# Another form of the seven products for the second MLP product: four sums instead of five, four banks instead of three, 21 quarters by seven

## The chip, the cores and the metric

The kernel runs on one core of one Trainium2 chip. The metric is the device time of one execution in microseconds; lower is better. TensorE does the matrix products, VectorE (DVE) and ScalarE (ACT) the elementwise work, GpSimd (POOL) and SyncE (SP) issue the transfers. A matrix product is written to one of eight accumulation banks (PSUM), each of 2 KB per partition, which is 512 float32 values; ACT and DVE read the banks.

## The reference, cut to what matters

```python
scores = scale * q @ k.T                     # 8 batches, 8 heads, 576 positions, 64 wide
ret    = scores * gamma ** (i - j)           # for i >= j, else 0; gamma by head
x      = (ret @ v), heads side by side       # 4608 tokens x 512
h      = x @ w_in                            # 512 x 2048
g      = 0.5 * h * (1 + erf(h / sqrt(2)))
out    = g @ w_out                           # 2048 x 512, float32
```

## The kernel before, in words

The 4608 tokens are nine blocks of 512. For each block the attention part gives `x` (by chunks of 128 positions with a running state), the first MLP product gives `h`, the gelu gives `g`, and the second MLP product gives the output. All weights stay in SBUF as bf16; `q`, `k`, `v` are loaded chunk by chunk through POOL's queue in the order of the list `ORDER`, and outputs are stored through SP's queue.

Some products are done "by seven": a product of 2 x 2 sub-blocks needs eight sub-products, and Strassen's scheme in Winograd's form needs seven, with sums of the inputs before and sums of the products after. The second MLP product is done so for blocks 1 to 8 (function `fast`): rows are cut into two halves of 256 tokens, columns into two halves of 256, and each of the seven products is two pieces, one for each 128 rows `r`, of eight matmuls of 256 columns. The two pieces of a product write the two halves of one bank, a tile of 128 x 2 x 256 float32; only in the last block has each row a bank of its own (`rows_at_once`). The first MLP product of a block is four quarters (`kp`), and a quarter is done plainly ("p" in `LAYOUTS`, 16 matmuls of 512 columns in `mlp1`) or by seven (a digit in `LAYOUTS`, 28 matmuls of 256 columns in `unit`). In `LAYOUTS` of before, blocks 2 to 8 have 2, 3, 2, 3, 2, 3 and 3 quarters by seven, 18 in all, and 10 plain ones.

In the second product of before, the products run in the order 3 2 1 5 4 6 7 on three banks Y, Z and X. Five sums of `g` (`g_sum`, ten DVE instructions a block) and five sums of `w_out` (`w_sum`, once) come before. After them `add_chain` puts a chain: product 3 is copied to SBUF (`third`), product 2 is taken from it (`less`), product 1 added (`more`), product 5 taken away (`dif`), and the four quadrants of the output are copied (`quadrant`) or added (`c11`) into the output buffer `o_sb`. Every one of these steps waits for both rows of a product, and reads the bank as 128 x 512 in one instruction.

The order of the instructions on each engine is fixed before the run by a planner written into the kernel (`Plan`, `pe_candidates`). It gives every operation a duration, a due time and what it depends on, and emits operations in the order of their planned start; TensorE's stream of MLP pieces may be taken out of order within a look-ahead of `LOOK` pieces, and attention work is put between them. The kernel sets no semaphore itself: the tile framework, in manual order, puts in the waits that the order of emission and the tiles touched call for. For the first 16 us the planner fills TensorE's gaps with matmuls on zeros (`warm`).

Of the kernel before, what the change touches and what calls it, by code (L numbers as in the profile page):

```python
# [9 lines left out]
FP32 = mybir.dt.float32  # L10
# [88 lines left out]
def kernel(  # L99
# [31 lines left out]
    for bp in range(B // 2):  # L131
        for ci in range(0 if bp > 1 else 1, NCI - 1):
# [12 lines left out]

    N_PE_TR = 10
    N_LD = 8
    N_QKT = 6
    N_VH = 5
    N_RET = 3  # L150
    N_Q = 3
    VH_ACT = [5, 8, 9, 10, 16, 18, 20, 24, 25, 29, 30, 33, 34, 37]
    HOT = 9.2
    N_WARM = 8
    SLACK = 0.05
    CUTS = (0, 128, 256, 384, 512)
    AHEAD = 5
    VH_DUE = 14.0
    FAST = 1
    UNIT_FROM = 2  # L160
    LOOK = 6
    HOLD = 4.7
    LAYOUTS = {2: ['2p3', '0', 'p1'], 3: ['0', '12', 'p3'], 4: ['01', 'p2', 'p3'], 5: ['0', '12', 'p3'], 6: ['32', 'p0', 'p1'], 7: ['01', '2', 'p3'], 8: ['0', '12', 'p3']}
    LEAD = 18.0
    SPREAD = 4.4
    EASE = 8.9
    ORDER = ("pos k1 q2 q1 k2 q3 v1 k3 v2 wi0 wi4 v3 q5 wi1 wi5 q4 wi2 wi6 wi3 k5 k4 wi7 wo0 v4 v5 wo4 wo1 wo5 k6 "
             "wo2 wo6 k9 q9 v8 k7 wo7 wo3 q7 q6 k10 v6 q8 v7 k8 q10 v9 v10").split()
    K_ORDER = [0, 1, 8, 9, 2, 3, 10, 11, 4, 5, 12, 13, 6, 7, 14, 15]
    PRODUCTS = "3215467"  # L170
    LAYOUT = {t: ["p0", "p1", "p2", "p3"] for t in range(2, N_BLK)}
    for t in range(UNIT_FROM, N_BLK):
        LAYOUT[t] = LAYOUTS[t]
# [80 lines left out]
    for t in range(N_BLK):  # L254
        if t < 2:
            cuts = CUTS if t == 0 else (0, 256, 512)
            for lo, hi in zip(cuts, cuts[1:]):
                stream.append([("1", t, m, 2, lo, hi) for m in K_ORDER[::2]])
        else:
            stream.append([one for block in LAYOUT[t] for one in laid(t, block)])  # L260
        if t < FAST:
            stream.append([("2", t, ts, m, m + 2) for m in range(0, N_DF, 2) for ts in range(2)])
            stream.append([("2", t, ts, m, m + 4) for ts in range(2, 4) for m in range(0, N_DF, 4)])
        else:
            stream.append([("2", t, p, r, n) for n, p in enumerate(PRODUCTS) for r in range(2)])

    def piece_time(one):
        if one[0] == "u":
# [398 lines left out]
    LEFT = {"2": 0, "1": 1, "5": 2, "6": 3, "7": 4}  # L667
    RIGHT = {"3": 0, "1": 1, "4": 2, "6": 3, "7": 4}
    BEHIND = {"5": "m3", "4": "q", "6": "dif", "7": "c21"}

    def g_of(t, m):
        kp = m % 8 // 2
# [7 lines left out]
    def g_sum(t, two, which):  # L680
        if which == 0:
            s_ring[two].take()
            s_tiles[t, two] = s_pool.tile([128, 3, 4, HALF], BF16, tag=f"s{two}", name="s")
        s_t = s_tiles[t, two]
        g = g_tiles[t, two].rearrange("p a b h s -> p (a b) h s")
        a11, a12 = g[:, :, 0, :HALF], g[:, :, 1, :HALF]
        a21, a22 = g[:, :, 0, HALF:], g[:, :, 1, HALF:]
        out_, x0, x1, op = ((s_t[:, 0], a21, a22, ALU.add), (s_t[:, 1], a11, a22, ALU.add),
                            (s_t[:, 2], a11, a12, ALU.add), (a21, a21, a11, ALU.subtract),
                            (a12, a12, a22, ALU.subtract))[which]  # L690
        nc.vector.tensor_tensor(out_, x0, x1, op=op)  # L691

    def w_sum(kp, which):
        if kp not in w_sums:
            w_sums[kp] = const.tile([128, 5, 2, 256], BF16, name=f"w_sum{kp}")
        hi, lo = w_out_sb[kp], w_out_sb[kp + 4]
        b11, b12, b21, b22 = hi[:, :, :256], hi[:, :, 256:], lo[:, :, :256], lo[:, :, 256:]
        x0, x1, op = ((b12, b22, ALU.subtract), (b11, b22, ALU.add), (b21, b11, ALU.subtract), (b11, b12, ALU.add),
                      (b21, b22, ALU.add))[which]
        nc.vector.tensor_tensor(w_sums[kp][:, which], x0, x1, op=op)  # L700

    for kp in range(4):
        for which in range(5):
            add(f"ws{kp}.{which}", "dve", 0.335, [f"land wo{kp}", f"land wo{kp + 4}"],
                lambda kp=kp, which=which: w_sum(kp, which), begins["2", FAST] - 6 + kp)

    def left(t, p, kp):
        if p in "215":
            return s_tiles[t, kp // 2][:, LEFT[p], kp % 2 * 2:kp % 2 * 2 + 2]
        g = g_tiles[t, kp // 2][:, kp % 2]  # L710
        return {"3": g[:, :, 0, :HALF], "4": g[:, :, 1, HALF:], "7": g[:, :, 1, :HALF], "6": g[:, :, 0, HALF:]}[p]

    def right(p, kp):
        if p == "2":
            return w_out_sb[kp][:, :, :256]
        if p == "5":
            return w_out_sb[kp + 4][:, :, 256:]
        return w_sums[kp][:, RIGHT[p]]


    wi_sums, xs_tiles, first_again = {}, {}, {}
# [92 lines left out]
    def chain_of(key, shape, n):  # L814
        c = chain.setdefault(key, {})
        if n not in c:
            c[n] = bank(shape, FP32, {"Y": "yT", "X": "xT_", "Z": "zT"}[n])
        return c[n][1]

    def unit(one):  # L820
# [14 lines left out]
    def fast(one):  # L835
        _, t, p, r, _ = one
        rs = next(x for x in rows_at_once(t) if r in x)
        c = chain_of(("2", t, rs), [128, len(rs), HALF], BANK_OF[p])
        at = r - rs[0]
        for kp in range(4):  # L840
            for kk in range(2):
                nc.tensor.matmul(c[:, at, :], lhsT=left(t, p, kp)[:, kk, r * 128:r * 128 + 128],  # L842
                                 rhs=right(p, kp)[:, kk, :], start=(p in "321" and at + kp + kk == 0),
                                 stop=(kp == 3 and kk == 1), skip_group_check=True)
        if p == PRODUCTS[-1] and r == 1:
# [59 lines left out]
    def c11(key):  # L905
        z = chain[key]["Z"][1]
        to = z if key[0] == "u" else target(key, "c11")
        nc.vector.tensor_tensor(to, chain[key]["q"], z, op=ALU.add)  # L908
        m_ring.give(T["dve"] + 0.12)
        if key[0] == "2":  # L910
            go(key, "Z", T["dve"] + 0.12)

    def add_chain(key, width, pe, due):

# [43 lines left out]
    for run in stream:  # L958
        for one in run:
# [18 lines left out]
            elif isinstance(one[2], str):  # L978
# [4 lines left out]
                if p in LEFT:  # L983
                    deps += [f"gs{t},{two}.{LEFT[p]}" for two in range(2)]
                if p in "34":
                    deps += gelus_of(t, range(4), int(p == "4"))
                deps += [f"ws{kp}.{RIGHT[p]}" for kp in range(4)] if p in RIGHT else []
                deps += [f"land wo{kp + 4 * (p == '5')}" for kp in range(4)] if p in "25" else []
                deps += [key + BEHIND[p]] if p in BEHIND else []
                add(nm, "pe", piece_time(one), deps, lambda one=one: fast(one), W[one], DRAIN,  # L990
                    banks=int(p in "321" and r == rs[0]))
                if p == PRODUCTS[-1] and r == rs[-1]:
                    at_ = {q_: {x: W["2", t, q_, x, PRODUCTS.index(q_)] for x in rs} for q_ in PRODUCTS}
                    add_chain(("2", t, rs), len(rs), {q_: [f"mlp{('2', t, q_, x, PRODUCTS.index(q_))}" for x in rs] for q_ in PRODUCTS},
                              {q_: max(at_[q_].values()) for q_ in PRODUCTS})
                    if t < N_BLK - 1:
                        add(f"st{t},1", "sp", 1.1, [key + "c21", key + "c22"], lambda t=t: store(t, 1), W[one])
                        add(f"st{t},0", "sp", 1.1, [key + "c12", key + "c11"], lambda t=t: store(t, 0), W[one] + 1)
                    else:
                        add(f"st{t},1.{r}", "sp", 0.5, [key + "c21", key + "c22"],  # L1000
                            lambda t=t, r=r: store(t, 1, slice(None), (r,), ends=False), W[one])
                        add(f"st{t},0a.{r}", "sp", 0.5, [key + "c12"],
                            lambda t=t, r=r: store(t, 0, slice(256, 512), (r,), ends=False), W[one])
                        add(f"st{t},0.{r}", "sp", 0.5, [key + "c11"],
                            lambda t=t, r=r: store(t, 0, slice(0, 256), (r,), ends=False), W[one] + 1)
            else:
                _, t, ts, n0, n1 = one
                ms = K_ORDER[n0:n1]
# [10 lines left out]
    for t in range(FAST, N_BLK):  # L1019
        for two in range(2):  # L1020
            kps = [2 * two, 2 * two + 1]
            gl = gelus_of(t, kps, 0) + gelus_of(t, kps, 1)
            for which in range(5):
                add(f"gs{t},{two}.{which}", "dve", 0.6, gl + ([f"gs{t},{two}.{which - 1}"] if which else []),
                    lambda t=t, two=two, which=which: g_sum(t, two, which),
                    begins["p", t, "21567"[which]] - 1.5 + 0.6 * two,
                    at=s_ring[two].at if not which else None)
    for kp in ever:
        over = [f"mlp{o}" for o in W if o[0] == "2" and o[1] == 0]
# [104 lines left out]
    def begun(one):  # L1134
# [2 lines left out]
            return one[3] in "321" or BANK_OF[one[3]] in chain.get(one[:3], ())  # L1137
        if one[0] == "2" and isinstance(one[2], str):
            rs = next(x for x in rows_at_once(one[1]) if one[3] in x)
            return (one[2] in "321" and one[3] == rs[0]) or BANK_OF[one[2]] in chain.get(("2", one[1], rs), ())  # L1140
        return True

    def pe_candidates():
# [113 lines left out]
```

## Time and profile before

| what | value |
|---|---|
| time, median of 3 runs | 287.55 us (286.61 to 287.65) |
| the profiled execution's own time | 285.85 us |
| its span, first to last instruction | 284.0 us |
| mean granted TensorE clock | 0.998 |
| TensorE busy | 278.8 us, 98% |
| DVE busy | 230.7 us, 81% |
| ACT busy | 174.6 us, 61% |
| POOL busy | 110.2 us, 39% |

The profiled execution lies 1.70 us under the median of the runs, and 1.9 us of its own time lie outside its span. A busy TensorE is counted from the start of a matmul to the modelled end of it, and matmuls are pipelined, so the spacing of the matmuls says more than the busy share.

### The profile page before, as it was taken

How to read it: one execution, taken by the hardware profiler on the slowest of the kernel's cores; microseconds unless marked ns; L12 is line 12 of the kernel's file. 1: busy time of each engine (PE TensorE's matmuls, PEld its weight loads, DVE VectorE, ACT ScalarE, POOL GpSimd, SP SyncE). 2: the span in 40 equal slices, each digit the busy share in tenths (PEclk: the TensorE clock that was granted, in tenths of full speed). 3: DMA queues.
4: the chain of work that ended last, by engine and by line, in shares of the span. 5: the costliest groups of instructions: out<-in, count | busy, mean ns of one | idle time of the engine just before them, and what ended most of it. 6: DMA issues, size and time to landing. Idle time of an engine off the chain costs nothing.

```text
span 284.0 us, 7609 instructions
## 1 busy us (share of the span) xinstructions
PE 278.8 (98%) x3080; PEld 219.9 (77%) x3080; DVE 230.7 (81%) x442; ACT 174.6 (61%) x396; POOL 110.2 (39%) x139
## 2 busy tenths in 40 slices
PE   7999999999999999999999999999999999999995
PEld 2689757588887688868875888688858887788684
DVE  4951775799999996979978999799789869939871
ACT  8678624797268735685377627884688258326921
POOL 8967778983566373508106467050000000000000
PEclk9999999999999999999999999999999999999999
DMA  9999999999999999999927999998310040003013
GB/s 151 159 182 189 187 181 162 193 193 135 136 146 184 178 131 129 149 214 156 178 84 41 154 159 225 144 147 70 148 37 6 0 148 3 2 11 139 0 35 115
DMA packets 151939, 35.49 MB, mean 125 GB/s; under 512 B 140896, under 2 KB 147552, under 8 KB 151904
## 3 DMA queue, kind: packets, MB, share of 16 engines
q0 software_dynamic: 115792, 17.97, 99.5%
q1 hardware_dynamic: 35072, 16.78, 32.8%
q8 instruction: 24, 0.39, 0.6%
q10 hardware_dynamic: 1040, 0.26, 0.4%
q14 instruction: 11, 0.09, 0.1%
HBM read 36.70 MB, written 9.44 MB: 162 GB/s over the span
## 4 chain that ended last, share of the span: by engine, by line
PE 60%; DVE 0%; issue 0%; DVEq 0%
PE zT L842 12%; PE hT L783 10%; PE yT L842 7%; PE zT L825 7%; PE yT L825 5%; PE o_ps L536 2%; PE sc L500 2%; PE o_ps L572 2%; PE xT__4502 L842 1%; PE xT__3131 L842 1%; PE xT__4102 L842 1%; PE xT__2624 L842 1%; PE xT__3636 L842 1%; PE u_ps L550 1%; PE xT__2163 L842 1%; PE xT__4807 L842 1%
## 5 line engine op out<-in xcount | busy, mean ns | idle before, releaser
L783 PE MATMUL hT<-xT,w_in 128*128 128x128 bf16 (+2 forms) x544 | 68.1, 279 | 0.0
L790 ACT ACTIVATE g<-hT 128x512 bf16<-128x512 f32 (+1 forms) x88 | 44.9, 527 | 16.9 <-PE hT L783 15.2
L842 PEld LDWEIGHTS <-g 128*128 128x128 bf16 x512 | 49.7, 98 | 7.0 <-issue 0.3
L783 PEld LDWEIGHTS <-w_in 128*128 128x128 bf16 x544 | 42.3, 98 | 16.3
L842 PEld LDWEIGHTS <-s 128*128 128x128 bf16 x384 | 37.4, 98 | 4.3
L412 POOL DMA_DIRECT2D qk_ld<-in_q_dram x31 | 27.9, 900 | 31.2 <-PE u_ps L550 19.0
L825 PEld LDWEIGHTS <-wi_sum 128*128 128x128 bf16 x360 | 35.1, 98 | 5.9 <-issue 0.2
L511 DVE TENSOR_TENSOR ret<-sc,msk 128x512 bf16<-128x512 f32 x56 | 36.1, 679 | 4.0 <-PE sc L500 4.0
L412 POOL DMA_DIRECT2D v_ld<-in_v_dram x31 | 27.9, 899 | 14.2 <-DMA qk_ld<-in_q_dram 4.8
L691 DVE TENSOR_TENSOR s<-g 128x1024 bf16<-128x1024 bf16 x48 | 31.5, 681 | 0.3 <-ACT g L899 0.3
L412 POOL DMA_DIRECT2D qk_ld<-in_k_dram x31 | 28.0, 902 | 8.4 <-DMA v_ld<-in_v_dram 4.7
L842 PE MATMUL zT<-w_sum,g 128*128 128x256 bf16 x256 | 30.7, 273 | 0.0
L524 ACT ACTIVATE vh<-v_ld,dv 128x64 bf16<-128x64 bf16 x104 | 26.5, 336 | 0.1
L899 ACT ACTIVATE g<-zT 128x512 bf16<-128x512 f32 x36 | 21.1, 629 | 2.7 <-DVE zT L908 2.7
L464 ACT COPY o_sb<-yT 128x512 f32<-128x512 f32 (+1 forms) x9 | 4.8, 538 | 28.6 <-PE yT L842 21.7
L464 ACT CAST u_sb<-u_ps 64x512 bf16<-64x512 f32 x29 | 16.8, 579 | 7.9 <-PE u_ps L550 7.0
L691 DVE TENSOR_TENSOR g<-g 128x1024 bf16<-128x1024 bf16 x32 | 21.3, 680 | 0.0
L464 ACT COPY q<-yT 128x512 f32<-128x512 f32 (+1 forms) x22 | 12.1, 572 | 13.7 <-PE yT L825 8.6
L587 DVE TENSOR_TENSOR xT<-o_ps,dqT 128x512 bf16<-128x512 f32 x28 | 18.2, 680 | 1.8 <-PE o_ps L572 1.7
L878 DVE TENSOR_TENSOR q<-q,zT 128x512 f32<-128x512 f32 (+1 forms) x27 | 17.5, 661 | 2.3 <-PE zT L825 1.3
L462 DVE COPY qkT<-qk_ps 128x512 bf16<-128x512 bf16 x14 | 5.9, 423 | 16.2 <-PE qk_ps L475 16.2
L908 DVE TENSOR_TENSOR zT<-q,zT 128x512 f32<-128x512 f32 x18 | 11.9, 692 | 6.7 <-PE zT L825 3.6
(199 smaller groups left out, 479.9 us busy)
## 6 DMA issues: line engine op xcount, KB each, us to landing
out_dram<-o_sb SPq DMA_DIRECT2D x30, 256.0 KB, 3.8
qk_ld<-in_k_dram POOLq DMA_DIRECT2D x31, 128.0 KB, 9.1
qk_ld<-in_q_dram POOLq DMA_DIRECT2D x31, 128.0 KB, 8.5
v_ld<-in_v_dram POOLq DMA_DIRECT2D x31, 128.0 KB, 8.9
w_in<-in_moe_w_in_dram POOLq DMA_DIRECT2D x8, 256.0 KB, 8.4
w_out<-in_moe_w_out_dram POOLq DMA_DIRECT2D x8, 256.0 KB, 8.6
out_dram<-o_sb SPq DMA_DIRECT2D x12, 128.0 KB, 2.3
qk_ld<-in_k_dram POOLq DMA_DIRECT2D x8, 64.0 KB, 6.5
```

Source lines behind the costliest of these rows:

```text
L412: nc.gpsimd.dma_start(dst, src[2 * bp + j, :, ci * C:ci * C + C, :].rearrange("h s d -> s h d"))
L464: nc.scalar.copy(dst, src)
L511: nc.vector.tensor_tensor(r, t, by, op=ALU.mult)
L524: nc.scalar.activation(vh[:, h], loaded[i][1][:, h], AF.Copy, scale=dv[:, h, ci:ci + 1])
L587: nc.vector.tensor_tensor(dst, o, by, op=ALU.mult)
L691: nc.vector.tensor_tensor(out_, x0, x1, op=op)
L783: nc.tensor.matmul(hT[:, m, :], lhsT=w[:, cc, o:o + 128], rhs=x_of(t)[:, cc, lo:hi], start=(cc == 0), stop=(cc == N_DM - 1))
L790: nc.scalar.activation(g_of(t, m0)[:, m0 % 2:m0 % 2 + n, m0 // 8, lo:hi], hT, AF.Gelu)
L825: nc.tensor.matmul(c[:, m, :], lhsT=unit_left(kp, p, m)[:, cc, :], rhs=unit_right(t, p)[:, cc, :], start=(p in "321" and m + cc == 0), sto ...
L842: nc.tensor.matmul(c[:, at, :], lhsT=left(t, p, kp)[:, kk, r * 128:r * 128 + 128], rhs=right(p, kp)[:, kk, :], start=(p in "321" and at + ...
L878: nc.vector.tensor_tensor(q_, q_, chain[key]["Z"][1], op=ALU.subtract)
L899: nc.scalar.activation(target(key, what), chain[key][n][1], AF.Gelu)
```

## The change

The second MLP product gets another form of the seven products. The sums of `g` are four (eight DVE instructions a block) and the sums of `w_out` are four; products 1, 2 and 3 take `w_out` as it is. The order is 1 2 6 7 4 5 3 on four banks: A holds product 1 and then product 2 on top of it, B product 6 and then 5, C product 7 and then 4, D product 3. Product 1 is copied by ACT, row by row, to an SBUF tile, and product 7, row by row, into the output buffer; product 2 of a row is allowed after product 1 of that row has been copied, and product 4 of a row after product 7 of that row. Partial sums of the output are kept in `o_sb`, and three DVE instructions add banks to them. The layouts of the first product become 3 quarters by seven in each of the blocks 2 to 8, 21 in all, with 7 plain ones. Several numbers of the planner and the order of the loads change too.

```diff
-    N_QKT = 6
+    N_QKT = 7
-    N_Q = 3
-    VH_ACT = [5, 8, 9, 10, 16, 18, 20, 24, 25, 29, 30, 33, 34, 37]
+    N_Q = 4
+    VH_ACT = [4, 6, 9, 14, 17, 20, 25, 30, 34, 35, 37]
-    SLACK = 0.05
+    SLACK = 0.3
-    LOOK = 6
-    HOLD = 4.7
-    LAYOUTS = {2: ['2p3', '0', 'p1'], 3: ['0', '12', 'p3'], 4: ['01', 'p2', 'p3'], 5: ['0', '12', 'p3'], 6: ['32', 'p0', 'p1'], 7: ['01', '2', 'p3'], 8: ['0', '12', 'p3']}
-    LEAD = 18.0
-    SPREAD = 4.4
-    EASE = 8.9
-    ORDER = ("pos k1 q2 q1 k2 q3 v1 k3 v2 wi0 wi4 v3 q5 wi1 wi5 q4 wi2 wi6 wi3 k5 k4 wi7 wo0 v4 v5 wo4 wo1 wo5 k6 "
...
+    LOOK = 8
+    HOLD = 5.1
+    LAYOUTS = {2: ['10', '2', 'p3'], 3: ['0', '12', 'p3'], 4: ['2', '30', 'p1'], 5: ['0', '12', 'p3'], 6: ['0', '1', '2', 'p3'], 7: ['0', '1', '2', 'p3'], 8: ['0', '12', 'p3']}
+    LEAD = 15.0
+    SPREAD = 4
+    EASE = 9
+    ORDER = ("q2 k1 k2 pos q1 k3 q3 wi0 v1 v2 wi4 wi1 wi5 v3 k5 wi6 wi2 wo0 k4 wi3 wo4 q5 q4 wo1 wi7 wo5 v4 wo2 v5 "
...
-    PRODUCTS = "3215467"
+    PRODUCTS = "3251647"
+    SECOND = "1267453"
...
+    BANK2 = {"1": "A", "2": "A", "6": "B", "5": "B", "7": "C", "4": "C", "3": "D"}
+    BEHIND2 = {"2": "p1", "5": "u2", "4": "p7"}
+    OPENS = "1673"
...
-        out_, x0, x1, op = ((s_t[:, 0], a21, a22, ALU.add), (s_t[:, 1], a11, a22, ALU.add),
-                            (s_t[:, 2], a11, a12, ALU.add), (a21, a21, a11, ALU.subtract),
-                            (a12, a12, a22, ALU.subtract))[which]
+        out_, x0, x1, op = ((s_t[:, 0], a21, a22, ALU.add), (s_t[:, 1], s_t[:, 0], a11, ALU.subtract),
+                            (a21, a11, a21, ALU.subtract), (s_t[:, 2], a12, s_t[:, 1], ALU.subtract))[which]
...
-        x0, x1, op = ((b12, b22, ALU.subtract), (b11, b22, ALU.add), (b21, b11, ALU.subtract), (b11, b12, ALU.add),
-                      (b21, b22, ALU.add))[which]
-        nc.vector.tensor_tensor(w_sums[kp][:, which], x0, x1, op=op)
+        x0, x1 = ((b12, b11), (b22, t_[:, 0]), (b22, b12), (b21, t_[:, 1]))[which]
+        nc.vector.tensor_tensor(t_[:, which], x0, x1, op=ALU.subtract)
...
-        c = chain_of(("2", t, rs), [128, len(rs), HALF], BANK_OF[p])
+        c = chain_of(("2", t, rs), [128, len(rs), HALF], BANK2[p])
...
-                                 rhs=right(p, kp)[:, kk, :], start=(p in "321" and at + kp + kk == 0),
+                                 rhs=right(p, kp)[:, kk, :], start=(p in OPENS and at + kp + kk == 0),
...
+    def first_of(key, width, r):
+        if not r:
+            m_ring.take()
+            chain[key]["p1"] = f_pool.tile([128, width, HALF], FP32, tag="q", name="q", bufs=N_Q)
+        nc.scalar.copy(chain[key]["p1"][:, r], chain[key]["A"][1][:, r])
+
+    def onto(key):
+        x = chain[key]["B"][1]
+        nc.vector.tensor_tensor(x, x, chain[key]["p1"], op=ALU.add)
+        m_ring.give(T["dve"] + 0.12)
+
+    def out_of(key, n, what, rows=slice(None)):
+
+        nc.scalar.copy(target(key, what)[:, rows], chain[key][n][1][:, rows])
+        if what == "c11":
+            release(chain[key]["A"][0], T["act"] + 0.14)
+
+    def out_plus(key, n, what):
+        to = target(key, what)
+        nc.vector.tensor_tensor(to, to, chain[key][n][1], op=ALU.add)
+        release(chain[key][n][0], T["dve"] + 0.12)
...
+    def add_second(key, width, pe, due):
...
+        for r in range(width):
+            add(nm + f"p1{r}", "act", 0.285, [pe["1"][r]] + ([nm + "p10"] if r else []), lambda r=r: first_of(key, width, r),
+                due["1"] + 0.1, at=None if r else m_ring.at)
+            add(nm + f"p7{r}", "act", 0.285, [pe["7"][r]], lambda r=r: out_of(key, "C", "c22", slice(r, r + 1)), due["7"] + 0.1,
+                at=room(1))
+        p7 = [nm + f"p7{r}" for r in range(width)]
+        add(nm + "on", "dve", dve, pe["6"] + [nm + f"p1{r}" for r in range(width)], lambda: onto(key), due["6"] + 0.1)
+        add(nm + "c11", "act", act, pe["2"], lambda: out_of(key, "A", "c11"), due["2"] + 0.3, at=room(0))
+        add(nm + "u2", "act", act, [nm + "on"], lambda: out_of(key, "B", "c21"), due["6"] + 0.5, at=room(1))
+        add(nm + "u4", "act", act, pe["5"], lambda: out_of(key, "B", "c12"), due["5"] + 0.1, at=room(0))
+        add(nm + "c21", "dve", dve, pe["4"] + [nm + "u2"], lambda: out_plus(key, "C", "c21"), due["4"] + 0.1)
+        add(nm + "c22", "dve", dve, pe["5"] + [*p7, nm + "u4"], lambda: out_plus(key, "B", "c22"), due["5"] + 0.6)
+        add(nm + "c12", "dve", dve, pe["3"] + [nm + "u4"], lambda: out_plus(key, "D", "c12"), due["3"] + 0.1)
...
+                deps += [key + BEHIND2[p] + (str(r - rs[0]) if p != "5" else "")] if p in BEHIND2 else []
                 add(nm, "pe", piece_time(one), deps, lambda one=one: fast(one), W[one], DRAIN,
-                    banks=int(p in "321" and r == rs[0]))
+                    banks=int(p in OPENS and r == rs[0]))
```

In this listing `p1` and `p7` are the row copies, `on` adds the copied product 1 to bank B, `u2` and `u4` copy bank B before and after product 5, and `c11`, `c21`, `c22`, `c12` finish the quadrants.

More of the change, by code (lines that the diff above doesn't have):

```diff
@@ L160 @@
     UNIT_FROM = 2
-    LOOK = 6
-    HOLD = 4.7
-    LAYOUTS = {2: ['2p3', '0', 'p1'], 3: ['0', '12', 'p3'], 4: ['01', 'p2', 'p3'], 5: ['0', '12', 'p3'], 6: ['32', 'p0', 'p1'], 7: ['01', '2', 'p3'], 8: ['0', '12', 'p3']}
-    LEAD = 18.0
-    SPREAD = 4.4
-    EASE = 8.9
-    ORDER = ("pos k1 q2 q1 k2 q3 v1 k3 v2 wi0 wi4 v3 q5 wi1 wi5 q4 wi2 wi6 wi3 k5 k4 wi7 wo0 v4 v5 wo4 wo1 wo5 k6 "
-             "wo2 wo6 k9 q9 v8 k7 wo7 wo3 q7 q6 k10 v6 q8 v7 k8 q10 v9 v10").split()
+    LOOK = 8
[5 more added lines that the diff above has]
+    ORDER = ("q2 k1 k2 pos q1 k3 q3 wi0 v1 v2 wi4 wi1 wi5 v3 k5 wi6 wi2 wo0 k4 wi3 wo4 q5 q4 wo1 wi7 wo5 v4 wo2 v5 "
+             "wo6 wo7 q6 wo3 q8 q7 k9 q9 v6 k7 k6 k8 v7 v8 v9 k10 q10 v10").split()
     K_ORDER = [0, 1, 8, 9, 2, 3, 10, 11, 4, 5, 12, 13, 6, 7, 14, 15]
-    PRODUCTS = "3215467"
+    PRODUCTS = "3251647"
+    SECOND = "1267453"
     LAYOUT = {t: ["p0", "p1", "p2", "p3"] for t in range(2, N_BLK)}
@@ L264 @@
         else:
-            stream.append([("2", t, p, r, n) for n, p in enumerate(PRODUCTS) for r in range(2)])
+            stream.append([("2", t, p, r, n) for n, p in enumerate(SECOND) for r in range(2)])
     def piece_time(one):
@@ L694, in w_sum @@
         if kp not in w_sums:
-            w_sums[kp] = const.tile([128, 5, 2, 256], BF16, name=f"w_sum{kp}")
-        hi, lo = w_out_sb[kp], w_out_sb[kp + 4]
+            w_sums[kp] = const.tile([128, 4, 2, 256], BF16, name=f"w_sum{kp}")
+        hi, lo, t_ = w_out_sb[kp], w_out_sb[kp + 4], w_sums[kp]
         b11, b12, b21, b22 = hi[:, :, :256], hi[:, :, 256:], lo[:, :, :256], lo[:, :, 256:]
-        x0, x1, op = ((b12, b22, ALU.subtract), (b11, b22, ALU.add), (b21, b11, ALU.subtract), (b11, b12, ALU.add),
-                      (b21, b22, ALU.add))[which]
-        nc.vector.tensor_tensor(w_sums[kp][:, which], x0, x1, op=op)
+        x0, x1 = ((b12, b11), (b22, t_[:, 0]), (b22, b12), (b21, t_[:, 1]))[which]
+        nc.vector.tensor_tensor(t_[:, which], x0, x1, op=ALU.subtract)
+    G_SUM = {"5": 0, "6": 1, "7": 2, "3": 3}
+    W_SUM = {"5": 0, "6": 1, "7": 2, "4": 3}
     for kp in range(4):
-        for which in range(5):
-            add(f"ws{kp}.{which}", "dve", 0.335, [f"land wo{kp}", f"land wo{kp + 4}"],
+        for which in range(4):
+            add(f"ws{kp}.{which}", "dve", 0.335, [f"land wo{kp}", f"land wo{kp + 4}"] + ([f"ws{kp}.{which - 1}"] if which else []),
                 lambda kp=kp, which=which: w_sum(kp, which), begins["2", FAST] - 6 + kp)
     def left(t, p, kp):
-        if p in "215":
-            return s_tiles[t, kp // 2][:, LEFT[p], kp % 2 * 2:kp % 2 * 2 + 2]
+        if p in "563":
+            return s_tiles[t, kp // 2][:, "563".index(p), kp % 2 * 2:kp % 2 * 2 + 2]
         g = g_tiles[t, kp // 2][:, kp % 2]
-        return {"3": g[:, :, 0, :HALF], "4": g[:, :, 1, HALF:], "7": g[:, :, 1, :HALF], "6": g[:, :, 0, HALF:]}[p]
+        return {"1": g[:, :, 0, :HALF], "2": g[:, :, 1, :HALF], "4": g[:, :, 1, HALF:], "7": g[:, :, 0, HALF:]}[p]
     def right(p, kp):
[L714 to L718, printed above, removed]
+        if p in W_SUM:
+            return w_sums[kp][:, W_SUM[p]]
+        return {"1": w_out_sb[kp][:, :, :256], "2": w_out_sb[kp + 4][:, :, :256], "3": w_out_sb[kp + 4][:, :, 256:]}[p]
     wi_sums, xs_tiles, first_again = {}, {}, {}
@@ L816, in chain_of @@
         if n not in c:
-            c[n] = bank(shape, FP32, {"Y": "yT", "X": "xT_", "Z": "zT"}[n])
+            c[n] = bank(shape, FP32, {"Y": "yT", "X": "xT_", "Z": "zT"}.get(n, "oT"))
         return c[n][1]
@@ L842, in fast @@
                 nc.tensor.matmul(c[:, at, :], lhsT=left(t, p, kp)[:, kk, r * 128:r * 128 + 128],
-                                 rhs=right(p, kp)[:, kk, :], start=(p in "321" and at + kp + kk == 0),
+                                 rhs=right(p, kp)[:, kk, :], start=(p in OPENS and at + kp + kk == 0),
                                  stop=(kp == 3 and kk == 1), skip_group_check=True)
-        if p == PRODUCTS[-1] and r == 1:
+        if p == SECOND[-1] and r == 1:
             for two in range(2):
@@ L911, in c11, with room @@
             go(key, "Z", T["dve"] + 0.12)
+    def first_of(key, width, r):
[16 more added lines that the diff above has]
+    def add_second(key, width, pe, due):
+        nm = f"c{key}"
+        half = 0.5 if width == 1 else 1.0
+        act, dve = 0.07 + 0.43 * half, 0.07 + 0.53 * half
+        def room(h, t=key[1]):
+            return lambda: 0.0 if ("o", t, h) in fold else o_ring[h].at()
+        for r in range(width):
[11 more added lines that the diff above has]
+        add(nm + "c12", "dve", dve, pe["3"] + [nm + "u4"], lambda: out_plus(key, "D", "c12"), due["3"] + 0.1)
     def add_chain(key, width, pe, due):
@@ L982 @@
                 deps = []
[L983 to L989, printed above, removed]
-                add(nm, "pe", piece_time(one), deps, lambda one=one: fast(one), W[one], DRAIN,
-                    banks=int(p in "321" and r == rs[0]))
[L992 to L995, printed above, removed]
+                if p in G_SUM:
+                    deps += [f"gs{t},{two}.{G_SUM[p]}" for two in range(2)]
+                else:
+                    deps += gelus_of(t, range(4), int(p != "1"))
+                deps += [f"ws{kp}.{W_SUM[p]}" for kp in range(4)] if p in W_SUM else []
+                deps += [f"land wo{kp + 4 * (p != '1')}" for kp in range(4)] if p in "123" else []
+                deps += [key + BEHIND2[p] + (str(r - rs[0]) if p != "5" else "")] if p in BEHIND2 else []
+                add(nm, "pe", piece_time(one), deps, lambda one=one: fast(one), W[one], DRAIN,
+                    banks=int(p in OPENS and r == rs[0]))
+                if p == SECOND[-1] and r == rs[-1]:
+                    at_ = {q_: {x: W["2", t, q_, x, SECOND.index(q_)] for x in rs} for q_ in SECOND}
+                    add_second(("2", t, rs), len(rs), {q_: [f"mlp{('2', t, q_, x, SECOND.index(q_))}" for x in rs] for q_ in SECOND},
+                               {q_: max(at_[q_].values()) for q_ in SECOND})
                     if t < N_BLK - 1:
@@ L1001 @@
                             lambda t=t, r=r: store(t, 1, slice(None), (r,), ends=False), W[one])
[L1002 to L1005, printed above, removed]
+                        add(f"st{t},0a.{r}", "sp", 0.5, [key + "c11"],
+                            lambda t=t, r=r: store(t, 0, slice(0, 256), (r,), ends=False), W[one])
+                        add(f"st{t},0.{r}", "sp", 0.5, [key + "c12"],
+                            lambda t=t, r=r: store(t, 0, slice(256, 512), (r,), ends=False), W[one] + 1)
             else:
@@ L1022 @@
             gl = gelus_of(t, kps, 0) + gelus_of(t, kps, 1)
-            for which in range(5):
+            for which in range(4):
                 add(f"gs{t},{two}.{which}", "dve", 0.6, gl + ([f"gs{t},{two}.{which - 1}"] if which else []),
                     lambda t=t, two=two, which=which: g_sum(t, two, which),
-                    begins["p", t, "21567"[which]] - 1.5 + 0.6 * two,
+                    begins["p", t, "5673"[which]] - 1.5 + 0.6 * two,
                     at=s_ring[two].at if not which else None)
@@ L1139, in begun @@
             rs = next(x for x in rows_at_once(one[1]) if one[3] in x)
-            return (one[2] in "321" and one[3] == rs[0]) or BANK_OF[one[2]] in chain.get(("2", one[1], rs), ())
+            return (one[2] in OPENS and one[3] == rs[0]) or BANK2[one[2]] in chain.get(("2", one[1], rs), ())
         return True
```

## The prediction

> **What bounds the kernel now.** I read the page's first two parts, then the chain of waits in order of time, then TensorE's timeline through second products, then what ACT and DVE do beside them.
>
> The page: TensorE is busy nearly throughout, at the full clock; DVE is next.
>
> ```profile
> PE 278.8 (98%) x3080; PEld 219.9 (77%) x3080; DVE 230.7 (81%) x442; ACT 174.6 (61%) x396; POOL 110.2 (39%) x139
> PE   7999999999999999999999999999999999999995
> DVE  4951775799999996979978999799789869939871
> PEclk9999999999999999999999999999999999999999
> ```
>
> The chain of waits (start, length, what), from the second product of block 5 on:
>
> ```profile
> 152.41 3.45 PE hT L783 x16
> 157.79 1.75 PE yT L842 x16
> 159.54 1.75 PE zT L842 x16
> 161.28 1.75 PE xT__3131 L842 x16
> 163.03 1.75 PE yT L842 x16
> 164.78 1.75 PE zT L842 x16
> 166.52 1.75 PE xT__3131 L842 x16
> 168.27 1.75 PE zT L842 x16
> 170.45 0.44 PE zT L825 x4
> ```
>
> Each product follows the one before without a gap: 16 matmuls of 256 columns in 1.75 us are 0.109 us each, and 16 of 512 columns in 3.45 us are 0.216 each. So TensorE's matmuls, at their own pace, set the time; a DVE that is 12.16 us busy in the 12.40 us from 157.6 to 170.0 (the windows view) still keeps up. What lengthens TensorE's stream lengthens the kernel, and what relieves DVE alone brings nothing.
>
> The timeline of the last block, where each row of a product has its own bank:
>
> ```profile
> 268.13 1.91 PE L842 MATMUL yT<-w_sum,g 128*128 128x256 bf16 x16
> 269.20 0.37 ACT L464 COPY q<-yT 128x256 f32<-128x256 f32 x1 [0.28 <-PE yT L842]
> 269.87 1.91 PE L842 MATMUL zT<-w_out,s 128*128 128x256 bf16 x16
> 270.07 0.37 ACT L464 COPY q<-yT 128x256 f32<-128x256 f32 x1 [0.50 <-PE yT L842]
> ```
>
> Row 0's eighth matmul starts at 268.13 + 7 x 0.109 = 268.89; ACT begins its copy 0.31 us later and needs 0.37. It ends at 269.57, inside row 1's matmuls (to 269.87).
>
> The timeline of block 4, where two engines copy different halves of one bank, `u_ps`:
>
> ```profile
> 129.09 0.67 DVE L462 CAST u_sb<-u_ps 64x512 bf16<-64x512 f32 x1
> 129.40 1.05 PE L842 MATMUL yT<-w_sum,g 128*128 128x256 bf16 x8
> 129.80 0.58 ACT L464 CAST u_sb<-u_ps 64x512 bf16<-64x512 f32 x1 [0.25 <-DVE u_sb L462]
> 130.48 0.58 ACT L464 COPY q<-yT 128x512 f32<-128x512 f32 x1
> ```
>
> ACT sat idle 0.25 us and began 0.04 after DVE's end (129.76), although the two share no partition, only the bank and the output tile. And the copy of `yT`, a bank shared by two rows, came as one 128x512 after both. In before no engine reads a bank while TensorE is writing its other half.
>
> **Part by part.**
>
> *Quarters by seven, 18 to 21.* A plain quarter is 16 x 0.216 = 3.45 us, one by seven 28 x 0.109 = 3.05. All lie on TensorE: 3 x 0.40 = 1.2 us less. The second product keeps its 14 pieces of eight matmuls: 0.
>
> *Sums, chains, heads of `v`.* DVE loses two sums in each of eight blocks (about 0.60 us apart in a run of them: 9.6 us) and four of `w_out` (0.42 each, 1.7); it gains three `vh` (1.8) and the four chain steps of three quarters (7.2): 2.4 us less. ACT gains in each of eight blocks four row copies of 0.37 for mostly one copy of 0.58 (about 7 us) and the quarters' copies (3), and loses three `vh` of 2.0: 4 us more on 174.6. Neither is on the path; cover is TensorE's own work. If DVE became late, the next to wait would be product 6 on the second sum, which now has 3.5 us of products 1 and 2 ahead of it where product 2 had 1.75 us ahead: it gets easier. I take 0.
>
> *The row copies.* This is the term that decides. In blocks 1 to 7 product 1 writes its rows into two halves of one bank A, and the planner, counting each row by itself, emits row 1's matmuls (planned at row 0's end) ahead of row 0's copy (planned 0.21 later). Waits follow the emitted order. If they are kept by bank, as between the two readers of `u_ps`, then ACT's copy of row 0 waits for row 1's last matmul, and product 2 row 0, next on TensorE, waits for that copy. Then row 1's copy, emitted behind product 2 row 0, which writes the same bank, waits for those matmuls, and product 2 row 1 for the copy. Products 7 and 4 on bank C do the same. So TensorE stops four times a block. Price of a stop: 0.31 (last matmul to ACT) + 0.37 (copy) + 0.04 (engine to engine, the `u_ps` row) = 0.72 between matmuls that would be 0.11 apart: 0.61 us. The bounds are 0, where a copy runs beside the other row as in the last block, and 0.61 + 0.58 = 1.19, where ACT first finishes a 128x512 copy. I take 0.61: ACT waits for the same row and is idle by then, being some 40% busy here (5.15 of those 12.40 us). Queued behind a waiting copy on ACT are gelus, `u_sb` copies and `vh` of attention, which are needed microseconds later; behind the waiting matmuls is all of TensorE. Seven blocks give 28 stops. Before, attention groups stand between pieces of the second product in blocks 1 (twice), 2, 4 and 6, five in all; such a group can cover a stop if it falls there. I take two of 28 as covered: 26 x 0.61 = 15.9 us more. Product 5 behind `u2` waits for a DVE add (0.69) and a copy (0.58) with products 7 and 4 (3.5 us) between: nothing. The last block has a bank for each row: nothing.
>
> The Trainium skill, "PSUM — Partial Sum Buffer", section "PSUM bank collisions raise a hardware error", says that two engines must be kept apart by bank and quadrant of 32 partitions, not by address: a ScalarE read beside a TensorE write in other columns of the bank counts. That rule speaks against splitting the copy by rows; by it the term stays 15.9, and without it would be 0. The trace is stricter than the rule: the two halves of `u_ps` lie in different quadrants and ACT waited all the same.
>
> *Four banks for three.* Attention needs two banks for `sc`, one for `o_ps` and the held `u_ps`, with eight in all. If a group found none, it would wait for a DVE step of 0.69 once a block, 4.8 us in all; I take 0, since TensorE can go on with first-product pieces.
>
> *Loads and the start.* `wi0` moves two places ahead in POOL's queue (rows 0.87 us apart, 1.7 us), `v1` and `v2` behind it, `pos` to fourth; each transfer's issue stays. TensorE's work up to 15.99 us is mixed with filler matmuls, which one or two pieces of the first product (8 x 0.056 = 0.45 us each) could replace, and which a late `v1` could prolong as much: -0.9 to +0.9, taken as 0.
>
> *The end.* The last step is again a 128x256 DVE add (0.42) and a store: 0.
>
> Sum: 15.9 - 1.2 = 14.7. The profiled execution goes from 285.85 to 300.55; it lies 1.70 under the median, so 287.55 + 14.7 = 302.2.
>
> **Rivals.** *Not slower: the row copies overlap.* If waits are kept by the columns touched, the copy of row 0 ends 0.31 + 0.37 + 0.04 = 0.72 us after its last matmul's start, inside row 1's 0.87. Only the quarters count: 287.55 - 1.2 = 286.3, at most 0.9 either way. For it: the last block's rows. Against it: the `u_ps` pair. It decides from the point at which the stops come below 1.2 / 28 = 0.04 us each. Chance 0.12.
>
> *Half of the stops covered.* The planner may take other pieces between (its look-ahead grows from 6 to 8 pieces) or put attention there: 13 x 0.61 - 1.2 = +6.7, 294.3. Against it: the planner does not know of the stop, and finds the next row ready. Chance 0.14.
>
> *ACT late at the stops.* Right at 157.6 to 170 ACT has groups of four or eight `vh` activations (about 1.0 and 2.0 us); if half the stops stood behind one piece of 0.58: 13 x 0.58 = 7.5 on top, 309.8. Chance 0.08.
>
> **How the numbers follow.** The forecast has 0.66: between 21 and 28 stops, 12.8 to 17.1, with 0.9 of the start either way, it runs from 298.3 to 304.4. With the covered case (0.14) 0.8 are in the range if it begins just under 294.3: 293.5 to 305.5. About 0.5% (1.4 us) is what a measurement of this kernel can tell from no change. Slower has 0.66 + 0.14 + 0.08 = 0.88; the overlap case, at -1.2 with 0.9 either way, is shared between faster and same, 0.06 each.
>
> **What would show it.** In the changed profile: product pieces on banks A and C as runs of eight matmuls with gaps of about 0.6 us before them, ended by ACT's copies of 128x256, four to a block and none in the last block; ACT's first row copy starting after the second row's last matmul, not the first's. 504 + 84 = 588 matmuls on `unit`'s line and 48 fewer of 512 columns. DVE's share falls from 81%. The forecast is wrong if the runs of 16 remain joined at 1.75 us, or the copies begin inside the other row.

## The result, and the profile after

The changed kernel takes 298.44 us (median of 6 runs, 297.94 to 298.73) where the kernel before, timed beside it, takes 287.51 (286.61 to 287.76): a ratio of 1.0384, with a 95% interval of 1.0367 to 1.0402, or 10.9 us more. The profiled executions are 298.15 and 285.85 us, 12.3 apart.

The page of the changed kernel, its busy times, TensorE's share in 40 slices, and the engines' shares of the chain that ended last:

```profile
PE 280.8 (95%) x3115; PEld 223.3 (75%) x3115; DVE 236.1 (80%) x445; ACT 173.8 (59%) x393; POOL 110.3 (37%) x139
PE   7999999998899999998999989999998899989994
PE 91%; ACT 3%; DMA 2%; issue 2%; DVE 1%; POOL 0%; ACTq 0%; POOLq 0%
```

TensorE is busy 2 us more in a span that is 12 us longer, and its slices drop to 8 in places where before they were 9 throughout. ACT now has 3% of the chain; in the page of before, whose chain is followed back over the last 60% of the span, it has none. The chain of waits in order of time, in the second product of block 1 (start, length, what; the rows "issue" of 0.02 to 0.04 us between them are left out):

```profile
68.54 1.76 PE oT L846 x16
70.32 0.38 ACT q L921
70.75 1.05 PE oT L846 x8
71.81 0.38 ACT q L921
72.24 1.91 PE oT L846 x16
```

This is the predicted pattern. Both rows of product 1 run (x16); only then is row 0 copied, although its own eight matmuls ended some 0.9 us earlier; product 2 row 0 runs (x8), then row 1 is copied, then product 2 row 1 runs. The sixteenth matmul of product 1 starts at 70.01, the next matmul at 70.75: 0.73 where 0.11 is the pace, so the stop costs 0.62. The view of the waits counts these stops:

```profile
PE oT L846 <- ACT o_sb L930: 5.2, 11, 0.5
PE oT L846 <- ACT q L921: 4.3, 9, 0.5
```

These are 9 stops before product 2 and 11 before product 4, 0.46 to 0.52 us idle each. Idle time begins at the modelled end of a matmul, 0.27 after its start, so 0.16 of the lost pace is not in it. By the spacing of the matmuls' starts the 20 stops cost 0.62 to 0.68 each, 12.9 us together. In blocks 1 to 7 there are 4, 2, 3, 3, 1, 4 and 3 of them.

The other eight of the 28 places are covered. TensorE's timeline in block 2 shows both ways:

```profile
103.48 1.03 PE L846 MATMUL oT<-w_out,g 128*128 128x256 bf16 x8 [0.46 <-ACT q L921]
104.44 0.64 PE L537 MATMUL o_ps<-ret,vh 128*64 128x128 bf16 x16
106.05 1.04 PE L846 MATMUL oT<-w_out,g 128*128 128x256 bf16 x8
111.04 1.03 PE L846 MATMUL oT<-w_sum,g 128*128 128x256 bf16 x8 [0.46 <-ACT o_sb L930]
111.91 1.04 PE L846 MATMUL oT<-w_sum,s 128*128 128x256 bf16 x8
112.78 1.04 PE L846 MATMUL oT<-w_sum,g 128*128 128x256 bf16 x8
```

Between the two rows of product 2 (103.48 and 106.05) stands an attention group, and between the rows of product 4 (111.04 and 112.78) stands a piece of product 5; neither second row waits.

In the last block each row has its own bank. The timeline there has the copies beside 32 matmuls without a gap:

```profile
279.88 3.66 PE L846 MATMUL oT<-w_out,g 128*128 128x256 bf16 x32
281.01 0.37 ACT L921 COPY q<-oT 128x256 f32<-128x256 f32 x1 [0.33 <-PE oT L846]
281.83 0.37 ACT L921 COPY q<-oT 128x256 f32<-128x256 f32 x1 [0.45 <-PE oT L846]
```

### The profile page after: what moved, and what is told of

The parts are those of the page before. It is cut to its first block, busy times and chain, and to the rows that moved or that the text cites. A ratio compares the mean times of both kernels' runs of the same rounds, so it can differ in the third digit from the quotient of the medians.

```text
span 296.2 us, 7673 instructions
## 1 busy us (share of the span) xinstructions
PE 280.8 (95%) x3115; PEld 223.3 (75%) x3115; DVE 236.1 (80%) x445; ACT 173.8 (59%) x393; POOL 110.3 (37%) x139
## 4 chain that ended last, share of the span: by engine, by line
PE 91%; ACT 3%; DMA 2%; issue 2%; DVE 1%; POOL 0%; ACTq 0%; POOLq 0%
PE oT L846 33%; PE hT L787 18%; PE zT L829 9%; PE yT L829 6%; PE oT L804 5%; PE o_ps L537 4%; PE sc L501 4%; PE o_ps L573 3%; DMA qk_ld<-in_q_dram 2%; PE qk_ps L476 2%; ACT o_sb L930 1%; PE u_ps L551 1%; PE warm L1170 1%; ACT q L921 1%; ACT q L465 0%
## 5 line engine op out<-in xcount | busy, mean ns | idle before, releaser
L787 PE MATMUL hT<-xT,w_in 128*128 128x128 bf16 (+2 forms) x496 | 57.4, 269 | 0.0
L794 ACT ACTIVATE g<-hT 128x512 bf16<-128x512 f32 (+1 forms) x76 | 37.8, 509 | 18.6 <-PE hT L787 17.3
L930 ACT COPY o_sb<-oT 128x256 f32<-128x256 f32 (+1 forms) x43 | 19.8, 478 | 48.8 <-PE oT L846 41.1
L787 PEld LDWEIGHTS <-w_in 128*128 128x128 bf16 x496 | 37.7, 98 | 11.9
L829 PEld LDWEIGHTS <-wi_sum 128*128 128x128 bf16 x420 | 41.0, 98 | 7.1 <-issue 0.4
L846 PE MATMUL oT<-w_sum,g 128*128 128x256 bf16 x256 | 31.3, 272 | 5.2 <-ACT o_sb L930 5.2
L846 PE MATMUL oT<-w_out,g 128*128 128x256 bf16 x256 | 31.5, 272 | 4.3 <-ACT q L921 4.3
L936 DVE TENSOR_TENSOR o_sb<-o_sb,oT 128x512 f32<-128x512 f32 (+1 forms) x27 | 16.8, 627 | 20.5 <-issue 7.1
L846 PE MATMUL oT<-w_sum,s 128*128 128x256 bf16 x256 | 31.2, 273 | 0.0
L522 DVE TENSOR_TENSOR vh<-v_ld,dv 128x512 bf16<-128x512 bf16 x26 | 17.8, 686 | 0.4 <-DMA v_ld<-in_v_dram 0.4
L829 PEld LDWEIGHTS <-w_in 128*128 128x128 bf16 x168 | 16.4, 98 | 2.1
```

The costliest lines, as they stand in the source:

```text
L522: nc.vector.tensor_tensor(vh, loaded[i][1], dv[:, :, ci:ci + 1].to_broadcast([128, H, D]), op=ALU.mult)
L787: nc.tensor.matmul(hT[:, m, :], lhsT=w[:, cc, o:o + 128], rhs=x_of(t)[:, cc, lo:hi], start=(cc == 0), stop=(cc == N_DM - 1))
L794: nc.scalar.activation(g_of(t, m0)[:, m0 % 2:m0 % 2 + n, m0 // 8, lo:hi], hT, AF.Gelu)
L829: nc.tensor.matmul(c[:, m, :], lhsT=unit_left(kp, p, m)[:, cc, :], rhs=unit_right(t, p)[:, cc, :], start=(p in "321" and m + cc == 0), sto ...
L930: nc.scalar.copy(target(key, what)[:, rows], chain[key][n][1][:, rows])
L936: nc.vector.tensor_tensor(to, to, chain[key][n][1], op=ALU.add)
```

## The experiments

The theory: the stops come from two rows sharing a bank, so that a row's copy and the other row's matmuls are kept apart. The main rival: the copy, or ACT's queue, holds up the next product whatever the bank.

**A bank for each row of product 1 (`rows_a`), then of products 1 and 7 (`rows_ac`).**

```diff
+    OWN = "A"        # rows_ac: "AC"
...
-        c = chain_of(("2", t, rs), [128, len(rs), HALF], BANK2[p])
+        own = BANK2[p] + (str(r) if BANK2[p] in OWN and len(rs) > 1 else "")
+        c = chain_of(("2", t, rs), [128, 1 if own[1:] else len(rs), HALF], own)
...
-        nc.scalar.copy(chain[key]["p1"][:, r], chain[key]["A"][1][:, r])
+        nc.scalar.copy(chain[key]["p1"][:, r], of_row(key, "A", r))
...
```

> Product 1 (and product 2 on top of it) of blocks 1 to 7 gets a bank for each row, bank C stays shared; order and copies are as in the changed kernel. Theory (a row's copy waits for the other row because both lie in one bank): the 9 stops before product 2 go, 9 x 0.63 = 5.7 us, from 298.4 to about 292.7, while the 11 stops before product 4 stay. Rival (the copy itself, or ACT's place in the queue, holds up the next product whatever the bank): stops and time stay, 298.4 within 0.5.

> Banks A and C both get a bank for each row, six banks in place of four; the copies of c11 and the adds of c21 become two of half the width. Theory (shared bank): all 20 stops go, 12.9 us, to about 285.5, which is below the kernel before (287.5). Rival (copy or ACT's queue): 298.4 within 0.5. Second rival (attention finds no bank and waits once a block for a DVE step of 0.69): 285.5 + 4.8 = 290.3.

Measured: `rows_a` 292.89 us against 292.7 expected; its ratio to before is 1.0215 (1.018 to 1.025), so by the ratios 4.9 us are gained where 5.7 were worked out. Its profile has no stop before product 2 in any block and still 11 before product 4. `rows_ac` 286.68 us against 286.83 of the kernel before on the same chip, ratio 0.9996 (0.9978 to 1.0014): all 20 stops are gone. The timeline of `rows_ac` in block 1, with the same copies of the same size on the same engine:

```profile
69.33 3.66 PE L848 MATMUL oT<-w_out,g 128*128 128x256 bf16 x32
70.41 0.37 ACT L927 COPY q<-oT 128x256 f32<-128x256 f32 x1 [0.28 <-PE oT L848]
71.28 0.37 ACT L927 COPY q<-oT 128x256 f32<-128x256 f32 x1 [0.50 <-PE oT L848]
```

The copy of row 0 now starts at 70.41, 0.32 after that row's eighth matmul (69.33 + 7 x 0.109 = 70.09), beside the matmuls of row 1, and the four pieces are one run of 32. The rival fell. The two rows' sharing of a bank is what cost the time: 11.2 us by the ratios (1.0384 less 0.9996, times 287.5), 12.9 by the spacing of the matmuls in the one profiled execution. The Trainium skill, "PSUM — Partial Sum Buffer", section "PSUM bank collisions raise a hardware error", asks for a guard by bank and quadrant and not by address. The waits in these traces agree with it: with the other row in other columns of the same bank row 0's copy began 1.18 us after the start of that row's eighth matmul (70.32, and 70.01 - 8 x 0.109 = 69.14), with the other row in another bank 0.32 after it. The waits were put in by the framework; what the chip does without them no run here shows.

One thing stays open. In this kernel every bank holds one tile, so a bank for each row is also a tile for each row, and the runs can't tell whether the waits go by the bank or by the PSUM tile. In SBUF they don't go by the whole tile: from 72.57 to 73.87 DVE writes one part of `s` while product 6 (from 73.11) reads another.

`rows_ac` did not come to the 285.5 that its expectation had. The second rival of that expectation, attention short of banks, is not what is left of it: among TensorE's waits in `rows_ac` none is for DVE, apart from the one before the first filler. What is left is looked at below.

**One copy for both rows (`whole`).**

```diff
-        for r in range(width):
-            add(nm + f"p1{r}", "act", 0.285, [pe["1"][r]] + ([nm + "p10"] if r else []), lambda r=r: first_of(key, width, r),
-                due["1"] + 0.1, at=None if r else m_ring.at)
...
+        add(nm + "p1", "act", act, pe["1"], lambda: first_of(key, width), due["1"] + 0.1, at=m_ring.at)
+        add(nm + "p7", "act", act, pe["7"], lambda: out_of(key, "C", "c22"), due["7"] + 0.1, at=room(1))
...
```

> One 128x512 copy after both rows of product 1 and of product 7 in place of two row copies, and the planner is told so. Theory (shared bank, so that row copies come one after the other with a stop each): two stops a block of 0.31 + 0.59 + 0.04 - 0.11 = 0.83 where there were up to four of 0.63; at most 14 x 0.83 = 11.6, and fewer where the planner, which now counts the wait, puts other pieces between; so between 287 and 297, faster than the changed kernel's 298.4 though each copy is longer. Rival (row copies hide part of the wait): slower than 298.4.

Measured: 289.19 us, ratio 1.0092 (1.0057 to 1.0128): by the ratios 8.4 us faster than with row copies. Three stops are left in the whole execution, at these places of TensorE's timeline:

```profile
71.10 1.91 PE L846 MATMUL oT<-w_out,g 128*128 128x256 bf16 x16 [0.67 <-ACT q L920]
78.81 1.91 PE L846 MATMUL oT<-w_sum,g 128*128 128x256 bf16 x16 [0.82 <-ACT o_sb L929]
218.57 1.03 PE L846 MATMUL oT<-w_out,g 128*128 128x256 bf16 x8 [0.67 <-ACT q L920]
```

Two of the stops cost 0.67 + 0.16 = 0.83, as worked out, and one 0.98. The planner, which now knows of the wait, puts other pieces or attention there at 11 of 14 places. This suggests that much of the changed kernel's loss is that the planner did not have the wait in its costs. It isn't shown alone: the run also has half as many places and longer copies, and no run keeps the row copies and tells the planner of the bank.

**Another product between (`order`).**

```diff
-    SECOND = "1267453"
+    SECOND = "1627543"
-                    begins["p", t, "5673"[which]] - 1.5 + 0.6 * two,
+                    begins["p", t, "6673"[which]] - 1.5 + 0.6 * two,
```

> The changed kernel with shared banks as they are, but the products in the order 1 6 2 7 5 4 3, so that another product (1.75 us, on another bank) stands between 1 and 2 and between 7 and 4; the first sums of g are due earlier. Theory (a stop is hidden when 0.72 us of other matmuls stand between): the 12.9 us go; product 6 now needs four sums 1.75 us after product 1 begins, not 3.5, which may cost up to 0.7 a block: 285.5 to 290.5. Rival (the copy holds TensorE up whatever stands between): 298.4.

Measured: 290.9 us, ratio 1.0116 (1.0077 to 1.0155), 0.4 above the upper end of what was expected. The stops before product 4 are all gone, but four of those before product 2 are left, where the planner takes product 2 first after all, as if product 6 were not ready by its sums. Two waits are new, 0.7 us for a gelu and 0.4 for a sum. In block 5 product 1 row 1 and product 2 row 0 are one run, and product 2 row 1 stops:

```profile
189.16 1.91 PE L846 MATMUL oT<-w_out,g 128*128 128x256 bf16 x16
191.53 1.03 PE L846 MATMUL oT<-w_out,g 128*128 128x256 bf16 x8 [0.46 <-ACT q L921]
```

**The copies done twice (`twice`).**

```diff
-        nc.scalar.copy(chain[key]["p1"][:, r], chain[key]["A"][1][:, r])
+        for _ in range(2):
+            nc.scalar.copy(chain[key]["p1"][:, r], chain[key]["A"][1][:, r])
```

and likewise for the copies of product 7.

> The changed kernel with each row copy of products 1 and 7 done twice in a row on ACT. Theory (the copy stands in TensorE's path at 20 stops): 20 x 0.33 to 0.37, so 6.6 to 7.4 us more than 298.4, 305 to 305.8. Rival (the stop is a wait for something else, and ACT has room): 298.4 to 299.

Measured: 308.02 us, ratio 1.072 (1.0673 to 1.0767), 9.6 us over the changed kernel. The dose went fully into TensorE's path, with 2.2 us more than the upper end of what was expected. ACT's and TensorE's timelines:

```profile
70.31 0.78 ACT L922 COPY q<-oT 128x256 f32<-128x256 f32 x2 [1.15 <-PE oT L846]
71.14 1.03 PE L846 MATMUL oT<-w_out,g 128*128 128x256 bf16 x8 [0.86 <-ACT q L922]
```

Two copies take 0.78 where one takes 0.37, so a stop grows from 0.62 to 1.03; 20 x 0.41 = 8.2, and places that had been covered begin to show (0.83 at 207 us, 0.36 at 115 us).

**The quarters alone, in the old form (`before21`) and in the new one (`rows_ac18`).**

```diff
 # before21: the kernel before, with the changed kernel's line LAYOUTS (21 quarters by seven)
 # rows_ac18: rows_ac, with the line LAYOUTS of the kernel before (18 quarters by seven)
```

> The kernel before, its second product unchanged, with the changed kernel's layouts: 21 quarters by seven, not 18. Theory of the prediction (TensorE's stream is all that counts): 1.2 us faster than before, 286.3. Rival (with five sums of g DVE can't carry three more quarters; it was 12.16 of 12.40 us busy in a second product): 7.2 us more DVE work of which up to half falls on the path, 288.5 to 292.

> Banks of their own for the rows of A and C, and the layouts of before: 18 quarters by seven in place of 21; all else as changed. Theory (the quarters are worth what their matmuls take, 1.0 to 1.2 us): 287.7 to 287.9 against 286.7. Rival (the gain of three more quarters is lost on DVE or to banks): 286.7 or less.

Measured: `before21` 289.97 us, ratio 1.0107 (1.0076 to 1.0138): 3.1 us slower than before, not 1.2 faster; its rival was right. In its timeline, at the second product of block 4:

```profile
159.05 1.89 DVE L691 TENSOR_TENSOR s<-g 128x1024 bf16<-128x1024 bf16 x3
161.46 1.27 DVE L587 TENSOR_TENSOR xT<-o_ps,dqT 128x512 bf16<-128x512 f32 x2
162.18 1.03 PE L842 MATMUL zT<-w_out,s 128*128 128x256 bf16 x8 [0.82 <-DVE xT L587]
```

TensorE waits 0.82 us before product 2 for a DVE that is behind. The wait ends with the first of the two `xT` steps (161.46 to 162.13), which reads attention's bank `o_ps` and stands in DVE's queue behind three sums of `g` and a copy. Three such waits before product 2 make 2.0 us, and the trace has 1.1 for a transposed load besides. `rows_ac`, with four sums and 21 quarters, has no wait for DVE there. That the fifth sum is the reason is argued and not shown: `rows_ac` also differs in the order, the banks and the planner's numbers, while `before21` has those that were set for 18 quarters. `rows_ac18` gives 287.41 us beside 287.09 of before, ratio 1.0003 (0.9979 to 1.0027), and `rows_ac` 0.9996: the 0.2 us between them are inside the intervals, so the gain of three quarters was not measured as time. What the quarters take of TensorE can be read from the spacing of the matmuls: 48 matmuls of 512 columns fewer (35.21 to 24.36 us) and 84 of 256 more in the two products (154.20 to 164.06) make 1.0 us less.

**Where that 1.0 us goes (`load10`, `tuned1`, `tuned3`, `rows_ac_b`).** In the profile of `rows_ac` the last matmul starts 1.15 us later than in that of before. Two items were found: fillers at the start (4.77 us, 3.74 before), and one wait of attention for a transposed load:

```profile
PE sc L501 <- DMA qkT<-qk_ld: 0.9, 1, 0.9
```

```diff
-    ORDER = ("q2 k1 k2 pos q1 k3 q3 wi0 v1 v2 wi4 wi1 wi5 v3 k5 ...
+    ORDER = "pos k1 q2 q1 k2 q3 v1 k3 v2 wi0 wi4 wi1 wi5 v3 k5 ...
 # tuned1, tuned3 besides: later loads, LAYOUTS, VH_ACT, SPREAD, HOLD, and LOOK and EASE or LEAD set anew, and
-        T["now"] = turned[0] + 3.4
+        T["now"] = turned[0] + 3.4 + (1.5 if i in (12, 13, 14) else 0.0)
```

> The kernel with banks of their own for the rows of A and C, and of the list of loads the first ten as before (pos k1 q2 q1 k2 q3 v1 k3 v2 wi0), the rest as changed. Theory (the new order of the first loads costs time at the start: filler matmuls of 4.77 us in place of 3.74 before the unbroken stream begins): 1.0 us less than the 286.7 of that kernel, 285.7. Rival (the start is hidden, and the loads as a whole set the pace): 286.7.

> Banks of their own for the rows of A and C, the first ten loads as before, and the planner told that the transposed loads of attention units 12 to 14 land 1.5 us later than it had them; later loads, layouts (still 21 quarters by seven) and spacing of attention set anew for that. Theory (what kept that kernel from the quarters' gain is the 0.9 to 1.4 us in which TensorE waits for the load of unit 14 at 80 to 82 us): the wait goes and the time falls by about that, 285.8 to 286.3 against 287.1 of the kernel before. Rival (loads set the pace up to there, and the wait comes back elsewhere): 287.

> A second setting of the same kind: loads nearly in the changed order behind the first ten, attention fetched 1 us earlier (16 in place of 15). Theory: as for the first setting, 285.8 to 286.3. Rival: 287.

> The kernel with banks of their own for the rows of A and C once more, beside the two settings on the same chip, with more rounds: 286.7 to 287.1, within 0.3% of the kernel before on either side.

Measured: `load10` 287.13 us, ratio 0.9998 (0.9971 to 1.0025); `tuned1` 286.23, 0.9994 (0.9968 to 1.002); `tuned3` 286.44, 0.9999 (0.9966 to 1.0033); `rows_ac_b` 286.60, 0.9986 (0.9962 to 1.001). None differs from before; the intervals reach 0.24 to 0.34% to either side, 0.7 to 1.0 us, so a gain of some tenths would not have been seen. In `load10` the fillers fell by 0.7 us and the extra spacing at the wait rose from 1.08 to 1.43; in `tuned1` it is still 1.14. In the profile of `tuned3` the wait is gone, and the time is the same. So the theory that these two items can be bought off one by one fell.

Nor are the items fixed. The second product of block 1 begins at 69.33 us in the profile of `rows_ac` and at 68.19 in that of `rows_ac_b`, which is the same kernel; in that of before it begins at 68.03. In `tuned3` TensorE takes 211.15 us from there to the start of the last matmul, 1.06 less than before (212.21), so the quarters' gain is in that stretch; but the stretch begins 1.03 later, at 69.06. Why it begins later was not found.

A third item is the end. The last addition and the stores that SP issues around it, first in before and then in the changed kernel:

```profile
279.20 2.22 SPq L942 DMA_DIRECT2D out_dram<-o_sb  x4
280.61 0.42 DVE L908 TENSOR_TENSOR o_sb<-q,zT 128x256 f32<-128x256 f32 x1 [0.45 <-PE zT L842]
291.42 2.23 SPq L990 DMA_DIRECT2D out_dram<-o_sb  x4
292.31 0.42 DVE L936 TENSOR_TENSOR o_sb<-o_sb,oT 128x256 f32<-128x256 f32 x1 [0.45 <-PE oT L846]
```

In before SP has issued its last store 0.39 us after the last addition (281.42 and 281.03), in the changed kernel 0.92 after it (293.65 and 292.73), because SP is still issuing the stores ahead of it. From the last addition to the end of the span it is 2.9 to 3.0 us in before and `before21`, and 3.4 to 3.5 in the profile of every kernel of the new form but `order`, which has 3.0. These 0.5 us were not worked on. No version tried beats the kernel before.

## Why the prediction was right, point by point

- **Direction, place and mechanism: right.** The stops are at products 2 and 4, in blocks 1 to 7 and not in the last, and ended by ACT's row copies; ACT's first copy starts after the second row's last matmul. Banks of their own remove them one bank at a time. Two labels in the reading of before are one too high: the second product at 157.79 is that of block 4 and the copies at 129 us stand in block 3, and two of the five attention groups lie in blocks 3 and 5, not 4 and 6. Nothing in the sum hangs on it.
- **Price of a stop: right.** 0.61 was worked out from 0.31, 0.37 and 0.04; 0.62 to 0.68 was measured.
- **Number of stops: too high.** The step "I take two of 28 as covered" failed: eight were covered, by attention groups and by pieces of other products. 20 x 0.645 = 12.9 us in place of 15.9. That is the term that was mis-sized, 3.0 of the 3.8 us between 302.2 and 298.4. Twenty stops are also fewer than the 21 to 28 from which the forecast's range of 298.3 to 304.4 was worked out; that the time lies at its lower end all the same is in part luck, since losses at the start and the end, both taken as 0, made up for 1.1 us.
- **From profile to median: 1.4 us off.** The step assumed that the changed kernel's profiled execution would lie as far under its median as that of before, 1.70; it lay 0.29 under. So +12.3 by profiles is +10.9 by medians. One execution of each kernel was profiled, so this difference can be chance.
- **Quarters: nearly right.** 1.2 was worked out, 1.0 is read from the matmuls' spacing. But "what relieves DVE alone brings nothing" holds for 18 quarters only: with 21 in the old form, `before21`, TensorE waits for DVE, and the kernel is 3.1 us slower.
- **Loads and the start: inside its bounds.** Fillers rose by 0.6 us (3.74 to 4.34), where 0 within 0.9 was taken.
- **The end: 0.5 us too low.** It was taken as 0; the last store is issued 0.5 us later behind the last addition.
- **DVE's and ACT's work: wrong sign, without effect seen.** For DVE 2.4 us less was worked out, and its busy time rose by 5.4 (230.7 to 236.1), with 445 instructions for 442. Most of that is seven more of the quarters' copies, about 0.69 us each, which went to it (12 on DVE, where it had 5). ACT, for which 4 us more was worked out, has 0.8 less (174.6 to 173.8).
- **The rivals.** "Not slower" gave 286.3 for copies that overlap; `rows_ac`, which makes them overlap, measured 286.7. "Half of the stops covered" came true in part: 8 of 28 were covered, between the 2 of the forecast and the 15 of this rival. "ACT late at the stops" didn't occur; the largest stop is 0.68.

## What to carry to other kernels

Halving a copy so that the next product can start sooner worked here only where the halves lay in different banks; on one bank the halved copy made two stops of 0.62 us where the whole one made one of 0.83. A planner that is written into a kernel should carry such a wait in its costs: told of it, it covered 11 of 14 places (with whole copies); not told, 8 of 28 (with halves). Before splitting work for an overlap, read from the trace whether the two sides have ever overlapped on that resource. And a gain on the busiest engine counts only if the kernel's start and end don't give it back.

## What the runs showed that was not expected

Even after the stops were removed and 1.0 us of matmuls saved, the time did not fall. One wait for a transposed load at about 81 us is part of what stands against the gain, and its length differs between executions of the same kernel: 0.9 us idle in the profile of `rows_ac`, and 2.8 in that of `rows_ac_b`, on TensorE's timeline:

```profile
83.83 0.40 PE L501 MATMUL sc<-qkT 64*128 64x128 bf16 x8 [2.82 <-DMA qkT<-qk_ld]
```

The profiled execution of `rows_ac_b` took 288.55 us where the median of its runs is 286.60, which is about what the longer wait would add (2.8 less 0.9); which executions have it was not settled.
